# Retention with a gated output unit: output weights in whole rows, the fourth unit's states earlier, and 81 more TensorE products that move the blocks of its program

## The chip, the cores and the metric

The kernel runs on one core of a Trainium2 chip. The metric is the device time of one execution in microseconds (us), and less is better. Engines are named as in the profile: PE is TensorE's stream of matrix products and PEld its stream of weight loads; DVE, ACT, POOL and SP are the vector, scalar, GpSimd and sync engines. SP only issues transfers here.

## The reference

Eight batches, eight heads, 576 positions, head size 64; all inputs and the output are float32.

```python
scores = q @ k.T / sqrt(64)
ret = scores * Dmat             # gamma_h ** (i - j) for i >= j, else 0
x = (ret @ v), heads side by side          # 8 x 576 x 512
gate = sigmoid(causal depthwise convolution of x, 5 taps, conv_w)
out = (gate * (x @ w_val)) @ w_out         # 512 x 512 weights
```

## The kernel before

The work is cut into 18 units. Unit 2b and unit 2b+1 are the first and second 256 positions of batch b; units 16 and 17 hold the last 64 positions of four batches each. A unit's retention is done in chunks of 128 positions: inside a chunk by scores and a mask, from chunk to chunk by a 64x64 state for each head.

For one unit the steps are these. `load_half` and `load1` bring k, q and v as float32 tiles (`fk`, `fq`, `fv`, or `wkc`, `wqc`, `wvc` for units 0, 1, 16 and 17). `cast1` and `cast_half` (L237 to L268) make bf16 of them, on POOL for the most part. `turn` or `turn_halves` (L287) transposes k and q on PE into PSUM, from where ACT copies them into `kq` (L297). `scores` (L306) multiplies them, `masks` (L324) applies the mask on DVE, `carried` (L352) adds what the states bring, `values` (L380) multiplies with v, and `take_x` (L392) writes x. `update` (L411) multiplies k and v into the unit's part of the states (L425); ACT copies it out (`xf`, L433), and POOL makes the bf16 states from it (`s`, L436 to L450; in second units through `mid`, L447). `conv` (L475) is the convolution, 40 products of 64x64 weights with 256 columns, and a sigmoid on ACT (L497). `value` (L505) is x times w_val, eight products of 128x128 weights with 256 columns (L510); `gated` multiplies with the gate (L517). `project` (L521) is the product with w_out, four products with 512 columns for one half of a unit's rows (L526); ACT copies its result to `ob` (L529), and `store` sends a unit out.

The order is written out by hand, and each engine runs its own instructions in that order. Units 0 to 3 have an order of their own (L572 to L730). From unit 4 on a loop over n (L731) interleaves three units: it finishes the retention of n, runs conv, gate_values and project of n-1, and begins n+1. In one round PE has, in this order: carried and the second half of scores of n (24 products together in first units, whose first chunk has no state, and 32 in second ones), conv(n-1) (40), the first half of scores of n+1 (16), update(n+1) (32), values(n) (32), two gate_values (16), turn_halves (16), two projects (8). Two rounds, a first and a second unit, have 376 products. Each product is a weight load and a multiplication, two instructions of PE's program.

PSUM has four pools: `ps_a`, `ps_s` and `ps_o` with one buffer each, and `ps_v` with two. A tile takes a buffer only when its last reader is done.

Loads are held back by a touch: a tiny copy by DVE or ACT into the tile (L112, L131, L136, L137), behind which the transfer has to wait, so that SP issues it when that engine has come so far. SP issues in order, so a transfer that waits holds all behind it.

The output weights come as two tiles `wof`, each by two transfers to 64 partitions (L134), in pieces of 128 floats; `prep_wo` (L225) makes bf16 of them by four casts on POOL. It stands ahead of `update(3)`, so POOL does the four casts ahead of the states of unit 3, which `carried(3, 0)` (L695) needs.

Of the kernel before, what the change touches and what calls it, by code (L numbers as in the profile page):

```python
# [21 lines left out]
def kernel(  # L22
# [55 lines left out]
    with tc.manual_schedule():  # L78
# [46 lines left out]
        wof = [consts.tile([P, NP, 2, P], F32, name=f"wof{g}") for g in range(2)]  # L125
# [8 lines left out]
        def load_wo(g, touch):  # L134
            wo_src = moe_w_out.rearrange("(pr ab hl p) (n j) -> ab hl p n pr j", pr=2, ab=2, hl=2, j=P)
            touch(wof[g][0:1, 0, 0, 0:1], lsc[0:1])  # L136
            touch(wof[g][64:65, 0, 0, 0:1], lsc[64:65])  # L137
            for (p0, ab, hl) in (((0, 0, 0), (64, 1, 0)), ((0, 1, 1), (64, 0, 1)))[g]:
                nc.sync.dma_start(out=wof[g][p0:p0 + 64], in_=wo_src[ab, hl])
# [70 lines left out]
        def prep_conv():  # L210
            cps = ps_a.tile([P, KC * NP], F32, name="a")
            nc.tensor.transpose(cps, cwn, identf[0:KC * NP, 0:KC * NP])
            cw = small.tile([P, KC * NP], F32, name="cw")
            nc.vector.tensor_copy(cw, cps)
            nc.vector.tensor_tensor(
                dg.rearrange("p o k j -> p k o j"),
                cw.rearrange("p (k o) -> p k o", o=NP).unsqueeze(3).to_broadcast([P, KC, NP, 64]),
                id2.unsqueeze(1).unsqueeze(1).to_broadcast([P, KC, NP, 64]), op=ALU.mult)

        def prep_wv(e, eng):  # L220
            for (j0, ab, hl) in (((0, 0, 0), (64, 1, 0)), ((0, 1, 1), (64, 0, 1)))[e]:
                for pr in range(2):
                    eng(wvb[e][:, :, pr, j0:j0 + 64], wvf[2 * pr + ab][:, :, hl * 64:hl * 64 + 64])

        def prep_wo():  # L225
            for o in range(NP):
                nc.gpsimd.tensor_copy(wob[:, o, :].rearrange("p (g j) -> p g j", j=P), wof[o // 2][:, :, o % 2, :])

        def warm(n, cols=512, pool=None):
            z = (pool or ps_v).tile([P, 512], F32, name="s" if pool else "v")  # L230
            for i in range(n):
                nc.tensor.matmul(z[:, 0:cols], lhsT=zero[:, 0:P], rhs=zero[:, 0:cols], start=True, stop=True)
# [44 lines left out]
        def turn(u, pool, i):  # L277

            new_turned(u)
            ps = tps[u, i] = pool.tile([P, 2, 2, 2, P], BF16, name="v" if pool is ps_v else f"o{i}")  # L280
            for hf in range(2):
                for prl in range(2):
                    for r in range(2):
                        h = 2 * (2 * hf + prl)
                        nc.tensor.transpose(ps[:, hf, prl, r, :], bf[u]["kq"[i]][:, r, h:h + 2, :].rearrange("p h d -> p (h d)"), ident)  # L285

        def turn_halves(*pairs):  # L287
            ps = ps_a.tile([P, 2, 2, 2, 2, P], BF16, name="a")
            for (at, (u, hf)) in enumerate(pairs):
                for i in range(2):  # L290
                    for prl in range(2):
                        for r in range(2):
                            h = 2 * (2 * hf + prl)
                            nc.tensor.transpose(ps[:, at, i, prl, r, :], bf[u]["kq"[i]][:, r, h:h + 2, :].rearrange("p h d -> p (h d)"), ident)  # L294
            for (at, (u, hf)) in enumerate(pairs):
                new_turned(u)
                nc.scalar.copy(kqt[u][hf].rearrange("p i l r c a -> p (i l r c a)"), ps[:, at].rearrange("p i l r a -> p (i l r a)"))  # L297
# [8 lines left out]
        def scores(u, hf, between=None, pool=None):  # L306

            if pool is ps_v:
                s = [pool.tile([P, 2, 2, P], F32, name="v") for par in range(2)]
            else:  # L310
                st = (pool or ps_s).tile([P, 2, 2, 2, P], F32, name="a" if pool else "s")
                s = [st[:, par] for par in range(2)]
            t = kqt[u][hf]
            for prl in range(2):
                for r in range(2):
                    for (c, par) in QUAD:
                        nc.tensor.matmul(s[par][half[c], prl, r, :], lhsT=t[half[par], 0, prl, r, c, :],  # L317
                                         rhs=t[half[par], 1, prl, :, c, :],
                                         start=True, stop=True, skip_group_check=True)
                    if between and prl == 0 and r == 0:  # L320
                        between()
            sps[u, hf] = s if pool is ps_v else st
# [29 lines left out]
        def carried(u, odd, chs=(0, 1)):  # L352
# [3 lines left out]
            for pr in range(NP):  # L356
                t = kqt[u][pr // 2]
                for c in chs:
                    par = c ^ odd
                    rows = half[par]  # L360
                    if kind == "full":
                        st = state.get((b, 2 * cu + c))
                        if st is None:
                            continue
                        nc.tensor.matmul(o[c][rows, pr, :], lhsT=st[rows, pr, :],  # L365
                                         rhs=t[rows, 1, pr % 2, :, c, :],
                                         start=first(u, c, par), stop=False, skip_group_check=True)
                    else:
                        for i in range(2):
                            st = state[b + 2 * c + i, 4]  # L370
                            cs = slice(i * 32, i * 32 + 32)
                            nc.tensor.matmul(o[c][rows, pr, :].rearrange("p (r a) -> p r a", r=2)[:, :, cs],
                                             lhsT=st[rows, pr, :], rhs=t[rows, 1, pr % 2, :, c, cs],
                                             start=first(u, c, par), stop=False, skip_group_check=True)
# [5 lines left out]
        def values(u, hf):  # L380
# [3 lines left out]
            for prl in range(2):  # L384
                pr = 2 * hf + prl
                for r in range(2):
                    for (c, par) in QUAD:
                        nc.tensor.matmul(o[c][half[par], pr, :], lhsT=vb[half[c], 2 * pr + par, r, :],  # L388
# [22 lines left out]
        def update(u, own=False):  # L411
# [9 lines left out]
            for pr in range(NP):  # L421
                for r in range(2):
                    for (c, par) in QUAD:
                        h = 2 * pr + par
                        nc.tensor.matmul(xy[c][half[par], pr * 64:pr * 64 + 64], lhsT=kb[half[c], r, h, :],  # L425
# [9 lines left out]

            s1 = stp.tile([P, NP, 64], BF16, name="s1")  # L436
# [16 lines left out]

# [21 lines left out]
        def conv(j, i, gate=True):  # L475
            n, ss = width(j), sets(j, i)
            g = ps_a.tile([P, 2, len(ss), n], F32, name="a")
            for si, s in enumerate(ss):
                a, b = 2 * s, 2 * s + 1
                for kk in range(KC):  # L480
                    for (rows, blk, cols, bank) in ((lo, a, lo, 0), (hi, b, lo, 1), (lo, b, hi, 0), (hi, a, hi, 1)):
                        nc.tensor.matmul(g[cols, bank, si, :], lhsT=dg[rows, blk, kk, :], rhs=xs(j, rows, blk, kk),  # L482
# [22 lines left out]
        def value(j, i, e):  # L505
            n, ss = width(j), sets(j, i)
            vp = ps_v.tile([P, len(ss), n], F32, name="v")
            for si, s in enumerate(ss):
                for o in range(NP):
                    nc.tensor.matmul(vp[:, si, :], lhsT=wvb[e][:, o, s, :], rhs=xs(j, slice(0, P), o, PAD),  # L510
# [10 lines left out]
        def project(j, m, r, eng=None):  # L521
            u = jobs[j][m]
            o = ps_v.tile([P, DM], F32, name="v")
            for jj in range(NP):
                z = zsb[j][:, jj, m * W:(m + 1) * W].rearrange("p (a r) -> p r a", r=2)
                nc.tensor.matmul(o, lhsT=z[:, r, :], rhs=wob[:, jj, :], start=(jj == 0), stop=(jj == NP - 1))  # L526
# [4 lines left out]
        def last_rows(j):  # L531
# [5 lines left out]
            for jj in range(NP):  # L537
                for r in range(2):
                    nc.tensor.matmul(o[r], lhsT=z[:, jj, r, :], rhs=wob[:, jj, :], start=(jj == 0), stop=(jj == NP - 1))
# [42 lines left out]
        load_wv(0)  # L582
        turn(0, ps_o, 0)
# [28 lines left out]
        load_wv(1, act)  # L612
# [4 lines left out]
        load_wv(2, dve)  # L617
        scores(1, 1, pool=ps_a)
        masks(1, 1)
        load_wv(3, dve)  # L620
        load_half("k", 3, 0, dve)
# [3 lines left out]
        load_half("k", 3, 1, act)  # L625
# [8 lines left out]
        load_half("q", 3, 0, dve)  # L634
# [3 lines left out]
        load_half("q", 3, 1, dve)  # L638
# [3 lines left out]
        load_half("v", 3, 0, dve)  # L642
# [3 lines left out]
        load_half("v", 3, 1, dve)  # L646
        scores(2, 1, pool=ps_v)
        load_wo(0, dve)
        masks(2, 1)
        load_wo(1, dve)  # L650
        prep_wv(0, pool)
        conv(1, 0)
        update(2)
        prep_wv(1, act)
# [16 lines left out]
        prep_wo()  # L671
        conv(2, 0)
        cast1("q", 3, act)
        gate_values(1, 0)
        load_half("v", 4, 0, dve)
        gate_values(1, 1)
        load_half("v", 4, 1, dve)
# [4 lines left out]
        load_half("k", 5, 0, dve)  # L682
        update(3)
        cast1("k", 4)
        gate_values(2, 0)
        load_half("q", 5, 0, dve)
        gate_values(2, 1)
        prep_tail_mask()
        load_half("v", 5, 0, dve)
# [4 lines left out]
        load_half("v", 5, 1, dve)  # L694
# [3 lines left out]
        load_half("k", 5, 1, dve)  # L698
        load_half("q", 5, 1, dve)
        project(0, 0, 0)  # L700
        project(0, 0, 1)
        store(0)
        project(1, 0, 0)
        values(3, 0)
        values(3, 1)
# [4 lines left out]
        load_half("k", 6, 0, dve)  # L710
        load_half("q", 6, 0, dve)
        turn_halves((4, 0))
        project(1, 0, 1)
        store(1)
        scores(4, 0)
        masks(4, 0)
        cast1("v", 5)
# [4 lines left out]
        load1("v", 6)  # L722
        turn_halves((4, 1), (5, 0))
        load_half("k", 6, 1)
        load_half("q", 6, 1)
        project(2, 0, 0)
        project(2, 0, 1)
# [3 lines left out]
        for n in range(4, NU):  # L731
# [34 lines left out]
            project(n - 1, 0, 0)  # L766
            project(n - 1, 0, 1)
# [35 lines left out]
```

## Time and profile before

| | |
|---|---|
| runs, without a profile | 162.41 us median of 3 (162.15 to 164.02) |
| the profiled execution, its own time | 164.84 us |
| its span, first to last instruction | 163.1 us |
| PE | 145.4 us busy, 3380 products |
| DVE, ACT, POOL | 105.5, 90.2, 103.1 us busy |
| transfers | 40.36 MB, 247 GB/s over the span |

The profiled execution lies 2.4 us above the median of the runs, and above the slowest of them. Its busy times are sums over stages with different limits. The span is longer than any engine's busy time, so what counts in each stage is which wait ends last.

### The profile page before, as it was taken

How to read it: one execution, taken by the hardware profiler on the slowest of the kernel's cores; microseconds unless marked ns; L12 is line 12 of the kernel's file. 1: busy time of each engine (PE TensorE's matmuls, PEld its weight loads, DVE VectorE, ACT ScalarE, POOL GpSimd, SP SyncE). 2: the span in 40 equal slices, each digit the busy share in tenths (PEclk: the TensorE clock that was granted, in tenths of full speed). 3: DMA queues.
4: the chain of work that ended last, by engine and by line, in shares of the span. 5: the costliest groups of instructions: out<-in, count | busy, mean ns of one | idle time of the engine just before them, and what ended most of it. 6: DMA issues, size and time to landing. Idle time of an engine off the chain costs nothing.

```text
span 163.1 us, 7863 instructions
## 1 busy us (share of the span) xinstructions
PE 145.4 (89%) x3380; PEld 107.9 (66%) x3380; DVE 105.5 (65%) x221; ACT 90.2 (55%) x160; POOL 103.1 (63%) x168
## 2 busy tenths in 40 slices
PE   6987978959999699996999999988999999999970
PEld 1556655835587578685769687867786877867530
DVE  4886896585466666665666676856676767664550
ACT  6795651816775528462847557474738483652420
POOL 7567764789969691969296959694949672400000
PEclk9999999999999999999999999999999999999997
DMA  4999899899999999897889898998899892303134
GB/s 125 347 346 341 252 299 231 240 295 304 323 341 354 330 324 289 250 316 216 250 255 305 270 285 253 300 274 284 227 244 277 227 285 113 133 4 133 26 103 129
DMA packets 64288, 40.36 MB, mean 247 GB/s; under 512 B 2410, under 2 KB 61822, under 8 KB 64254
## 3 DMA queue, kind: packets, MB, share of 16 engines
q1 hardware_dynamic: 64032, 39.59, 79.9%
q8 instruction: 26, 0.43, 1.2%
q10 hardware_dynamic: 222, 0.27, 0.7%
q14 instruction: 8, 0.07, 0.1%
HBM read 30.42 MB, written 9.44 MB: 244 GB/s over the span
## 4 chain that ended last, share of the span: by engine, by line
PE 72%; DVE 10%; issue 6%; DMA 3%; POOL 3%; SPq 2%; ACT 2%; DVEq 0%; POOLq 0%; ACTq 0%
PE v L510 19%; PE v L526 15%; PE a L482 10%; PE a L294 7%; PE o L388 4%; PE o L365 3%; PE s L425 3%; DVE p L334 3%; PE s L317 2%; SPq L97 2%; DMA wqc<-in_q_dram 2%; PE v L317 2%; DVE p L330 2%; PE o L285 1%; DVE xg L399 1%
## 5 line engine op out<-in xcount | busy, mean ns | idle before, releaser
L297 ACT COPY kq<-a 128x1024 bf16<-128x1024 bf16 x28 | 27.1, 1015 | 35.8 <-PE a L294 35.8
L510 PE MATMUL v<-xg,wvb 128*128 128x256 bf16 x288 | 35.2, 273 | 4.2 <-issue 3.9
L517 DVE TENSOR_TENSOR z<-gate,v 128x512 bf16<-128x512 f32 x34 | 23.3, 686 | 18.6 <-PE v L510 17.4
L334 DVE TENSOR_TENSOR p<-s,mask 128x1024 bf16<-128x1024 f32 x17 | 20.8, 1222 | 19.5 <-PE s L317 19.5
L510 PEld LDWEIGHTS <-wvb 128*128 128x128 bf16 x288 | 26.7, 97 | 9.5 <-issue 4.9
L526 PE MATMUL v<-wob,z 128*128 128x512 bf16 x136 | 32.4, 379 | 0.2 <-DVE z L517 0.2
L245 POOL TENSOR_TENSOR vb<-fv,gin 128x512 bf16<-128x512 f32 x28 | 28.7, 1044 | 2.5 <-DMA fv<-in_v_dram 2.4
L497 ACT ACTIVATE gate<-a 128x1024 f32<-128x1024 f32 x17 | 17.4, 1025 | 17.2 <-PE a L482 10.6
L482 PE MATMUL a<-xg,dg 64*64 64x256 bf16 x720 | 24.3, 270 | 0.6 <-DVE xg L399 0.3
L399 DVE TENSOR_TENSOR xg<-o,gout 128x512 bf16<-128x512 f32 x32 | 22.2, 735 | 3.3 <-PE o L388 2.6
L529 ACT COPY ob<-v 128x512 f32<-128x512 f32 x34 | 18.5, 582 | 4.5 <-PE v L526 4.5
L526 PEld LDWEIGHTS <-z 128*128 128x128 bf16 x136 | 12.3, 98 | 13.0 <-DVE z L517 1.3
L482 PEld LDWEIGHTS <-dg 64*64 64x64 bf16 x720 | 19.9, 106 | 1.4 <-issue 0.9
L317 PEld LDWEIGHTS <-kq 64*64 64x64 bf16 x576 | 15.5, 106 | 2.6 <-issue 1.8
L252 POOL CAST kb<-fk 128x512 bf16<-128x512 f32 x28 | 17.0, 613 | 0.0
L330 DVE TENSOR_TENSOR p<-v,mask 128x512 bf16<-128x512 f32 x24 | 15.5, 686 | 1.1
L447 POOL TENSOR_TENSOR mid<-run,xf 128x256 f32<-128x256 f32 x8 | 5.8, 725 | 15.3 <-ACT xf L433 13.6
L388 PE MATMUL o<-p,vb 64*64 64x128 bf16 x576 | 12.4, 218 | 1.8 <-DVE p L334 0.6
L252 POOL CAST qb<-fq 128x512 bf16<-128x512 f32 x22 | 13.5, 616 | 0.1
L317 PE MATMUL s<-kq 64*64 64x128 bf16 x304 | 12.2, 222 | 0.7 <-ACT kq L297 0.3
L388 PEld LDWEIGHTS <-vb 64*64 64x64 bf16 x576 | 9.8, 107 | 3.6 <-issue 3.2
L365 PEld LDWEIGHTS <-s 64*64 64x64 bf16 x192 | 7.0, 106 | 7.7 <-issue 2.5
(104 smaller groups left out, 201.7 us busy)
## 6 DMA issues: line engine op xcount, KB each, us to landing
out_dram<-ob SPq DMA_DIRECT2D x16, 512.0 KB, 5.0
fk<-in_k_dram SPq DMA_DIRECT2D x28, 256.0 KB, 4.4
fq<-in_q_dram SPq DMA_DIRECT2D x28, 256.0 KB, 4.9
fv<-in_v_dram SPq DMA_DIRECT2D x28, 256.0 KB, 4.9
wkc<-in_k_dram SPq DMA_DIRECT2D x2, 512.0 KB, 4.9
wqc<-in_q_dram SPq DMA_DIRECT2D x2, 512.0 KB, 5.4
wvc<-in_v_dram SPq DMA_DIRECT2D x2, 512.0 KB, 5.9
wvf<-in_moe_w_val_dram SPq DMA_DIRECT2D x4, 256.0 KB, 3.7
```

What stands on the lines that cost most here:

```text
L245: nc.gpsimd.tensor_tensor(b[n][:, hs].rearrange("p h r d -> p (h r) d"), f.rearrange("p h (r d) -> p (h r) d", r=2), gin[:, units[u][2], h ...
L252: (eng or nc.gpsimd.tensor_copy)(b[n][:, :, hs].rearrange("p r h d -> p h r d"), f.rearrange("p h (r d) -> p h r d", r=2))
L297: nc.scalar.copy(kqt[u][hf].rearrange("p i l r c a -> p (i l r c a)"), ps[:, at].rearrange("p i l r a -> p (i l r a)"))
L317: nc.tensor.matmul(s[par][half[c], prl, r, :], lhsT=t[half[par], 0, prl, r, c, :], rhs=t[half[par], 1, prl, :, c, :], start=True, stop=Tru ...
L330: nc.vector.tensor_tensor(p[:, par].rearrange("p l r a -> p l (r a)"), sps[u, hf][par].rearrange("p l r a -> p l (r a)"), mrow.to_broadcas ...
L334: nc.vector.tensor_tensor(p.rearrange("p e l r a -> p (e l) (r a)"), sps[u, hf].rearrange("p e l r a -> p (e l) (r a)"), mrow.to_broadcast ...
L388: nc.tensor.matmul(o[c][half[par], pr, :], lhsT=vb[half[c], 2 * pr + par, r, :], rhs=p[half[c], par, prl, r, :], start=first(u, c, par), s ...
L399: nc.vector.tensor_tensor(x[:, b, :, PAD + i0:PAD + i0 + P].rearrange("p o (a r) -> p o r a", r=2), o[c].rearrange("p o (r a) -> p o r a", ...
L482: nc.tensor.matmul(g[cols, bank, si, :], lhsT=dg[rows, blk, kk, :], rhs=xs(j, rows, blk, kk), start=(si == 0 and kk == 0), stop=(si == len ...
L510: nc.tensor.matmul(vp[:, si, :], lhsT=wvb[e][:, o, s, :], rhs=xs(j, slice(0, P), o, PAD), start=(si == 0 and o == 0), stop=(si == len(ss) ...
L517: nc.vector.tensor_tensor(zsb[j][:, 2 * e + ss[0]:2 * e + ss[-1] + 1, :], gsb[j, i][e], vps[j, i, e], op=ALU.mult)
L526: nc.tensor.matmul(o, lhsT=z[:, r, :], rhs=wob[:, jj, :], start=(jj == 0), stop=(jj == NP - 1))
```

## The change

Six things are changed.

1. The output weights are loaded as four tiles of 128 partitions, each row 512 floats long, and cast by ACT (two) and POOL (two). So that each block of 128 rows fits, the second bank of the convolution has its two blocks on the other partitions, and the order of a group of four conv products is now lower-lower, upper-upper, lower-upper, upper-lower. `prep_wv` follows.
2. `update` can leave its POOL part for later (`states`). For unit 3 that part now stands behind one cast of output weights instead of four.
3. `project` takes `split`: for the first `split` of its four weight blocks the 512 columns are done in two products of 256. All products are counted, and `fill()` adds small products on zeros (64 columns) until the count, with 16 added, leaves 50 when divided by 127.
4. Around unit 4 the order is another: `turn_halves` for (4, 0) comes before `project(1, 0, 0)`, in a `ps_v` buffer, and the one for (4, 1) and (5, 0) before scores(4, 0); `values(3, 1)` comes before `values(3, 0)`; the mask for the tail is made later.
5. Loads come earlier or without a touch in several places.
6. `prep_wv(1)`, the four casts of w_val on ACT, moves ahead of `conv(1, 0)`.

PE has 3461 products after it: 73 from splits and 8 from `fill()`. In the loop, `split` is 2 and 2 for even n and 2 and 1 for odd n, so that two rounds have 383 products.

```diff
-        wof = [consts.tile([P, NP, 2, P], F32, name=f"wof{g}") for g in range(2)]
+        wof = [consts.tile([P, DM], F32, name=f"wof{o}") for o in range(NP)]
...
+        def load_wo(o, touch=None):
+            if touch:
+                touch(wof[o][0:1, 0:1], lsc[0:1])
+            src = moe_w_out.rearrange("(pr ab hl p) n -> hl pr ab p n", pr=2, ab=2, hl=2)
+            nc.sync.dma_start(out=wof[o], in_=src[o // 2, o % 2])
+
+        made = [0]
+        BLOCK, PLACE = 127, 50
...
+        def fill():
+            z = ps_v.tile([P, 512], F32, name="v")
+            while (made[0] + 4 * NP) % BLOCK != PLACE:
+                matmul(z[:, 0:64], lhsT=zero[:, 0:P], rhs=zero[:, 0:64], start=True, stop=True)
...
-            for (j0, ab, hl) in (((0, 0, 0), (64, 1, 0)), ((0, 1, 1), (64, 0, 1)))[e]:
+            for (j0, ab, hl) in (((0, 0, 0), (64, 1, 0)), ((0, 0, 1), (64, 1, 1)))[e]:
...
-        def prep_wo():
-            for o in range(NP):
-                nc.gpsimd.tensor_copy(wob[:, o, :].rearrange("p (g j) -> p g j", j=P), wof[o // 2][:, :, o % 2, :])
+        def prep_wo(os, eng):
+            for o in os:
+                eng(wob[:, o, :], wof[o])
...
         def turn_halves(*pairs):
-            ps = ps_a.tile([P, 2, 2, 2, 2, P], BF16, name="a")
+            if len(pairs) == 1:
+                ps = ps_v.tile([P, 1, 2, 2, 2, P], BF16, name="v")
+            else:
+                ps = ps_a.tile([P, 2, 2, 2, 2, P], BF16, name="a")
...
+            xfs[u] = xf
+            if now:
+                states(u)
...
-                    for (rows, blk, cols, bank) in ((lo, a, lo, 0), (hi, b, lo, 1), (lo, b, hi, 0), (hi, a, hi, 1)):
+                    for (rows, blk, cols, bank) in ((lo, a, lo, 0), (hi, b, hi, 1), (lo, b, hi, 0), (hi, a, lo, 1)):
...
-                nc.tensor.matmul(o, lhsT=z[:, r, :], rhs=wob[:, jj, :], start=(jj == 0), stop=(jj == NP - 1))
+                n = DM // 2 if jj < split else DM
+                for c in range(0, DM, n):
+                    matmul(o[:, c:c + n], lhsT=z[:, r, :], rhs=wob[:, jj, c:c + n], start=(jj == 0 and c == 0),
+                                     stop=(jj == NP - 1), skip_group_check=True)
...
         masks(2, 0)
-        load_half("v", 3, 1, dve)
+        load_wo(0, dve)
+        load_wo(1)
         scores(2, 1, pool=ps_v)
-        load_wo(0, dve)
         masks(2, 1)
-        load_wo(1, dve)
+        load_wo(2, dve)
+        load_wo(3)
         prep_wv(0, pool)
+        prep_wv(1, act)
         conv(1, 0)
         update(2)
-        prep_wv(1, act)
...
-        prep_wo()
+        cast1("q", 3, act)
         conv(2, 0)
-        cast1("q", 3, act)
...
-        update(3)
+        update(3, now=False)
+        prep_wo((0, 1), act)
+        prep_wo((2,), pool)
+        states(3)
+        prep_wo((3,), pool)
         cast1("k", 4)
...
-        project(0, 0, 0)
-        project(0, 0, 1)
+        project(0, 0, 0, 4)
+        project(0, 0, 1, 4)
         store(0)
-        project(1, 0, 0)
+        turn_halves((4, 0))
+        project(1, 0, 0, 4)
+        values(3, 1)
         values(3, 0)
-        values(3, 1)
...
         update(4)
         take_x(3)
...
-        turn_halves((4, 0))
-        project(1, 0, 1)
+        turn_halves((4, 1), (5, 0))
+        project(1, 0, 1, 4)
         store(1)
         scores(4, 0)
...
-        turn_halves((4, 1), (5, 0))
...
-        project(2, 0, 0)
-        project(2, 0, 1)
+        fill()
+        project(2, 0, 0, 4)
+        project(2, 0, 1, 4)
...
-            project(n - 1, 0, 0)
-            project(n - 1, 0, 1)
+            project(n - 1, 0, 0, 2)
+            project(n - 1, 0, 1, 2 - n % 2)
```

## The prediction

> **What bounds the kernel now.** I read the page first, then the waits, the chain and timelines of single stretches.
>
> ```profile
> PE 145.4 (89%) x3380; PEld 107.9 (66%) x3380; DVE 105.5 (65%) x221; ACT 90.2 (55%) x160; POOL 103.1 (63%) x168
> ...
> PE 72%; DVE 10%; issue 6%; DMA 3%; POOL 3%; SPq 2%; ACT 2%; DVEq 0%; POOLq 0%; ACTq 0%
> ...
> q8 instruction: 26, 0.43, 1.2%
> ```
>
> PE sets the end: 72% of the chain is its work. The time to be won is where it stands still. Two kinds of stop stand out, the first in the waits:
>
> ```profile
> PEld L510 <- issue: 4.9, 5, 1.8
> PE v L510 <- issue: 3.9, 3, 1.6
> PEld L365 <- POOL s L448: 2.2, 1, 2.2
> PE o L365 <- POOL s L448: 2.0, 1, 2.0
> ```
>
> "issue" means that nothing the profile shows was waited for. Laid beside the transfers, these stops have an owner. Queue q8 fetches 26 times 16 KB, and the longest stops lie behind such a fetch, here one that ran from 55.07 to 56.03 us (timeline: start, us, what, and in brackets the idle time before):
>
> ```profile
> 55.40 0.28 PE L510 MATMUL v<-xg,wvb 128*128 128x256 bf16 x1
> 57.30 0.92 PE L510 MATMUL v<-xg,wvb 128*128 128x256 bf16 x7 [1.62 <-issue]
> ```
>
> Counting the products from one stop to the next (stretch, us, busy time and number by engine, clock, transfer share, GB/s):
>
> ```profile
> 57.30:74.71 17.41, 15.79 (x384) 12.41 (x384) 11.35 (x22) 9.24 (x18) 12.53 (x20) 1.00 0.92 290
> 74.71:106.49 31.78, 31.07 (x768) 24.50 (x768) 22.25 (x43) 18.48 (x36) 23.81 (x37) 1.00 0.87 267
> ```
>
> From the restart at 57.30 us to the one at 74.71 are 384 products, to the one at 106.50 another 768: multiples of 128 products, 256 instructions, so 64 bytes each for 16 KB. PE's program comes in blocks of 128 products, and PE stops where the next block is not there yet. Beyond the usual spacing the four stops of the loop cost 1.80 (57.30), 1.75 (74.71), 0.79 (106.50) and 0.59 us (111.60), 4.9 in all; one at 26.45 costs 0.9.
>
> How long a block needs: over 17 blocks of the loop, the fetch begins 0.9 to 2.8 us after the first product of the block before, moves for 0.88 to 2.53 us, and at the stops PE goes on 1.27 to 1.52 us after it landed. With 1.3 us for the last, the sum is 3.3 to 5.1 us, mean 4.4, spread 0.5. Where PE does 128 products faster, it stops. Seven scores products, conv, 16 scores, update, values and one value product are 128 in 2.6 us: the stop at 57.30.
>
> The second kind is the 2.24 us before 35.87 (POOL's timeline):
>
> ```profile
> 31.60 1.17 POOL L227 CAST wob<-wof 128x512 bf16<-128x512 f32 x2 [0.62 <-DMA wof<-in_moe_w_out_dram]
> 33.51 1.17 POOL L227 CAST wob<-wof 128x512 bf16<-128x512 f32 x2 [0.74 <-DVE fq L112]
> 34.64 0.72 POOL L447 TENSOR_TENSOR mid<-run,xf 128x256 f32<-128x256 f32 x1
> 35.42 0.40 POOL L448 CAST s<-mid 128x256 bf16<-128x256 f32 x1
> ```
>
> POOL casts all output weights and waits twice for them, while `xf` has been there since 32.38.
>
> **The change, part by part.** The sum is made against the profiled execution (164.84 us, span 163.1); its saving is then taken off the median of 162.41, which lies 2.4 lower.
>
> *States of unit 3.* After it, POOL does one cast (0.61), then `mid` (to the start of `s` 0.78) and `s` (0.40). `xf` allows `mid` from 32.4, so `s` is ready at about 33.6, when carried wants it (33.63): minus 2.2. If the third weight transfer lands where the fourth did (33.36), `s` comes at 35.2: minus 0.65. I take 2.0, because the transfers should be quicker. From 26 to 30 us all transfers together move 182 GB/s, from 46 to 54 338; in the slow stretch two of the four loads to 64 partitions are issued. With 128 partitions 4 us at the full rate would move 0.6 MB more, 1.8 us earlier for what follows.
>
> What is late next: ACT, whose next casts wait for q of unit 4.
>
> ```profile
> 35.20 0.62 ACT L252 CAST qb<-fq 128x512 bf16<-128x512 f32 x1 [2.81 <-DMA fq<-in_q_dram]
> 36.77 0.62 ACT L252 CAST qb<-fq 128x512 bf16<-128x512 f32 x1 [0.96 <-DMA fq<-in_q_dram]
> ```
>
> Its two weight casts (0.62 each) fit into the 2.81. But behind these casts stand the copies of `project` to `ob`, which free `ps_v`, which the moved turn_halves(4, 0) now needs, at about 36.1 (the first project at 36.66 less 2.2, and 1.73 for two). The touch for the second half of q is at 27.90, its transfer was issued at 31.12 and landed at 36.70; after the change it lands between 33.5 (touch plus 5.57 of flight) and 36.7. At 35 it costs about nothing.
>
> *Order around unit 4.* PE waited 0.47 us at 41.99 for a `kq` copy; turned earlier, the copy is there: minus 0.4. New small waits, on `ob` copies and on the casts of unit 5, whose cover shrinks from 2 us to 1: plus 0.3 (0 to 0.8).
>
> *Extra products.* A product of 256 columns follows the last every 108.4 ns (L510), one of 512 every 216 (L526): a split costs 1 ns if its weight load is hidden as in L510. 73 of them: plus 0.1. If the loads were not hidden, 73 x 98 ns = 7.2. The Trainium skill speaks against it: TensorE: Matmul & The Clock Gate, Part 3, says that a weight load overlaps a running product only when its row group differs, and all these have all rows. The 108.4 ns with a load before each product disagree, and the measurement decides. Eight fills of 64 columns: plus 0.2, by a quarter of 108.4 ns each.
>
> *Conv places.* 40 products take 1.04 to 1.12 us, 27 ns each, a quarter of 108.4: four blocks work at once already, before and after. Nothing, within 0.04 for each of 18.
>
> *Touches left out, `prep_wv` earlier.* DVE saves 0.25 us ahead of masks(2, 1), but the stop at 26.45 behind them is set by its fetch (landed 24.70) and swallows it. The ACT casts go into ACT's 2.8 us of idle before 22.2. Nothing; if that fetch is quicker, up to minus 1.2.
>
> *Blocks at other places.* Two rounds are now 383 products, three blocks less one, so the borders stay put: one in conv (product 27 to 32 of 40), one in project (product 3 to 8 of 12), one at the start of values. Without stops, by the durations before: conv to project 4.55 us, growing to 5.2; values to conv 6.2; project to values 4.03, 3.95, 3.85, 3.64, 3.44 in turn, since the border creeps by a product each time. The four old stops go, minus 4.9. New ones come where a block needs longer. One block in the trace before begins at project with loads running: its fetch is at 124.22 to 125.15, need 3.9; the mean of all is 4.4. I take 4.1 with the spread of 0.5, which gives stops of 0.24, 0.28, 0.35, 0.51 and 0.68 before values, 0.1 elsewhere: 2.2. Bounds: 0 and 8.2 (every block needs 5.1).
>
> Sum: -2.0 - 0.4 + 0.3 + 0.1 + 0.2 - 4.9 + 2.2 = -4.5 us. From 164.84 that is 160.3 with a profile, and 157.9 without.
>
> The rest of the loop has cover for a PE that is early: transfers are busy to 89%, and POOL waits 1.4 us or more in most rounds for ACT.
>
> **The rivals.**
>
> *PE's program is read far ahead.* Then a border in project, whose slow products leave time, costs nothing. For it: the fetch at 143.96 begins 0.44 us before its block's first product, in project too. Against: there transfers were nearly over, and blocks that begin in transposes still saw 2.3 and 2.6. New stops 0: 162.41 - 6.7 = 155.7. The Trainium skill gives TensorE a queue of 64 instructions (TensorE: Matmul & The Clock Gate, its first table), which favours this; the average lag of 1.7 us, against 2.1 right after a stop, shows only a little of it.
>
> *q of unit 4 still lands at 36.7.* The `ob` copies begin at 37.4 and turn_halves at 38.0 instead of 36.1: 1.9 of the 2.0 are lost, 159.8.
>
> *The stops are not the fetches' doing* and come back elsewhere: 162.41 - 1.8 = 160.6. The Trainium skill (Runtime: NRT & Kernel Launch, Instruction fetch mechanics) has crossing a 16 KiB border mostly hidden, which is this case. Against it stand five stops exactly at borders, each after a late fetch.
>
> *Fetches need 5.1 us, and the change is slower.* Blocks at 106.50 and 111.60 needed 5.0 to 5.1, with transfers running as they will in project. Then five borders before values cost 1.1 to 1.7 each and those in project 0.2 to 0.5: 8.2 for 4.9, and with -1.8 from the rest 163.9. It decides from a mean need of 4.93 on. Against: only four of 17 needed that much.
>
> *Split loads are not hidden:* 157.9 + 7.2 = 165.1. Against it stands L510.
>
> **How the numbers follow.** Forecast 0.45; read ahead 0.20; late q 0.13; fetch needs 5.1 0.14; stops not the fetches' 0.05; split loads 0.03. The likeliest is 157.9. Two per cent, about what a measurement of this kernel can tell from no change, is 159.2 below and 165.7 above. The forecast is below with 0.8, reading ahead with 0.95, late q with 0.3: 0.59 faster. Slower by over 2%: a quarter of the fetch case and half of the split case, some 0.05. The range goes from just under the read-ahead case to just under the slower one: 154.9 to 163.4.
>
> **What would show it.** In the changed profile PE should wait for `s` no more than 0.6 us near 34; products of 256 columns in project should be 108 to 110 ns apart; the stops called issue should lie at values, five of 0.2 to 0.7 us, and none at 1.5 or more in value. Stops over 1 us at values, or in project, would make the prediction wrong, as would a wait of turn_halves on `ob` near 36, or stops away from borders 128 products apart.

## The result: slower by 8.3%

| | before | after |
|---|---|---|
| median of 4 runs each | 163.22 us (162.15 to 164.30) | 176.96 us (176.50 to 180.15) |
| ratio, 95% interval | | 1.083 (1.072 to 1.0945) |
| span of the profiled execution | 163.1 us | 175.2 us |

Ratios here and below come from runs within 1.5% of the fastest of their kernel, so a median over all runs and its ratio can differ, by up to 1.2 per cent.

The prediction, 157.9 us, has the wrong sign, and 176.96 lies outside its range. The page of after, in the lines that answer to those shown of before, and with two rows of the 40 slices (4.4 us each):

```profile
PE 149.5 (85%) x3444; PEld 118.3 (68%) x3461; DVE 105.1 (60%) x214; ACT 92.3 (53%) x162; POOL 102.8 (59%) x166
...
PEclk9999999985557999999999999999999999999999
...
GB/s 142 347 346 334 292 238 58 55 75 136 200 296 309 319 308 317 320 295 299 290 254 291 299 281 272 282 273 263 315 232 235 232 262 245 67 68 121 7 120 120
...
q8 instruction: 27, 0.44, 1.1%
...
PE 71%; DVE 9%; SPq 5%; issue 5%; DMA 4%; POOL 3%; ACT 1%; POOLq 0%; ACTq 0%; DVEq 0%
```

From the seventh to the ninth slice, 26 to 39 us, the transfers fall from over 300 GB/s to 55 to 75; from the tenth slice to the twelfth PE's clock is at a half. SP's queue has 5% of the chain and transfers 4%, against 2% and 3% before. The waits of after (engine, line, releaser; sum, times, longest; every product has line 146 now, that of the counting wrapper):

```profile
PEld L146 <- issue: 16.5, 42, 1.4
...
POOL wob L242 <- DMA wof<-in_moe_w_out_dram: 14.6, 2, 11.8
ACT qb L267 <- DMA fq<-in_q_dram: 14.4, 3, 11.9
...
PEld L146 <- POOL s L475: 10.1, 1, 10.1
...
PE o L146 <- POOL s L475: 10.0, 1, 10.0
```

PE's wait for `s` of unit 3, 2.2 us before, is 10.0 us. POOL's timeline says why (start, us, what, idle before):

```profile
41.24 0.61 POOL L242 CAST wob<-wof 128x512 bf16<-128x512 f32 x1 [11.79 <-DMA wof<-in_moe_w_out_dram]
41.82 0.72 POOL L474 TENSOR_TENSOR mid<-run,xf 128x256 f32<-128x256 f32 x1
42.60 0.40 POOL L475 CAST s<-mid 128x256 bf16<-128x256 f32 x1
...
46.45 0.61 POOL L242 CAST wob<-wof 128x512 bf16<-128x512 f32 x1 [2.77 <-DMA wof<-in_moe_w_out_dram]
```

The states follow the third cast, as the change wants, and that cast waits for the third weight transfer, which was issued at 23.75 and landed at 41.12. Transfers behind it wait too, on SP's queue (the time is that of the issues):

```profile
22.39 10.52 SPq L138 DMA_DIRECT2D wof<-in_moe_w_out_dram  x4
33.00 7.41 SPq L113 DMA_DIRECT2D fk<-in_k_dram  x2
40.50 3.67 SPq L113 DMA_DIRECT2D fq<-in_q_dram  x2
```

Four transfers of 256 KB keep SP for 10.5 us, so k, q and v of unit 4 come 12.5 to 13.3 us later than before (the second half of q at 49.24 instead of 36.70). On PE this makes three stops in a row; two smaller ones of the loop, 60 us apart, stand below them:

```profile
43.05 0.42 PE L146 MATMUL o<-kq,s 64*64 64x128 bf16 x4 [9.99 <-POOL s L475]
...
47.11 2.29 PE L146 MATMUL v<-wob,z 128*128 128x256 bf16 x10 [1.18 <-POOL wob L242]
50.47 0.58 PE L146 MATMUL v<-ident,kb 128*128 128x128 bf16 x4 [1.07 <-ACT ob L558]
...
70.18 0.22 PE L146 MATMUL s<-vb,kb 64*64 64x64 bf16 x2 [0.86 <-issue]
...
130.77 0.63 PE L146 MATMUL o<-p,vb 64*64 64x128 bf16 x30 [0.51 <-issue]
```

The ledger of the two profiled executions: `carried(4, 0)` begins at 59.4 us instead of 45.1, 14.4 lost. The waits account for 10.0 + 1.2 + 1.1, less the 2.2 that PE waited for `s` before: 10.1. The rest, 4.3, is about what the half clock cost, at which PE came back from its 10 us of idling and ran until about 55 us: up to `carried(4, 0)` PE is busy for 42.5 us against 37.5, with 32 products more (stretch, us; busy time and number for PE, weight loads, DVE, ACT and POOL; clock, transfer share, GB/s; after, then before):

```profile
0.00:59.45 59.45, 42.46 (x813) 30.65 (x816) 30.19 (x83) 30.03 (x50) 33.19 (x63) 0.86 0.73 222
```

```profile
0.00:45.07 45.07, 37.54 (x781) 25.18 (x781) 30.84 (x90) 27.47 (x47) 33.59 (x64) 1.00 0.97 283
```

From `carried(4, 0)` to the end of the span, after takes 115.8 us and before 118.0: 2.3 less. This is not shown to be the change's doing, for the second profile of the unchanged kernel, at the end of the experiments, takes 115.8 there too.

**Why are these transfers slow?** For each of before's weight transfers the trace has 16 updates of its semaphore, one for each landing. For each of after's it has three: one as the transfer is issued (23.47, 24.08, 25.59 and 33.33 us), which would have to stand for 14 of the 16, and then two landings, at 30.51 and 30.82, 35.66 and 35.94, 40.85 and 41.12, 46.10 and 46.40: one transfer every 5.2 us. From 28 to 43 us some 2.1 packets of 2 KB are under way at any time. That is the picture of two DMA engines working for each transfer, one transfer after the other; which engines they are the trace does not tell. The source of a transfer has the dimensions 2 (`ab`), 64 and 512. The Trainium skill (DMA: Bandwidth & Descriptors, section "Why a DMA increments its semaphore by 16 and not by 1") has the rule for it: the hardware takes the largest number up to 16 that divides the slowest dimension of both sides, and the sequencer writes the counts of the engines left out at once. With a slowest dimension of 2 that makes two engines, and 14 counts at once: the trace agrees, with two landings and one update at the issue.

### The profile page after: what moved, and what is told of

Same layout as the page of the kernel before. It is cut to its first block, busy times and chain, and to the rows that moved or that the text cites. A ratio compares the mean times of both kernels' runs of the same rounds, so it can differ in the third digit from the quotient of the medians.

```text
span 175.2 us, 7992 instructions
## 1 busy us (share of the span) xinstructions
PE 149.5 (85%) x3444; PEld 118.3 (68%) x3461; DVE 105.1 (60%) x214; ACT 92.3 (53%) x162; POOL 102.8 (59%) x166
## 4 chain that ended last, share of the span: by engine, by line
PE 71%; DVE 9%; SPq 5%; issue 5%; DMA 4%; POOL 3%; ACT 1%; POOLq 0%; ACTq 0%; DVEq 0%
PE v L146 39%; PE a L146 16%; PE o L146 10%; PE s L146 7%; SPq L113 5%; DVE p L352 4%; DMA fq<-in_q_dram 4%; DVE p L348 1%; DVE z L543 1%; DVE xg L417 1%; DVE kq L319 1%; POOL vb L260 1%; POOL qb L267 1%; POOL kb L267 1%; DVE last L570 0%
## 5 line engine op out<-in xcount | busy, mean ns | idle before, releaser
L315 ACT COPY kq<-a 128x1024 bf16<-128x1024 bf16 x26 | 25.0, 1015 | 29.4 <-PE a L146 29.4
L146 PE MATMUL v<-wob,z 128*128 128x256 bf16 (+1 forms) x195 | 34.6, 317 | 2.5 <-POOL wob L242 1.2
L146 PEld LDWEIGHTS <-z 128*128 128x128 bf16 x217 | 21.3, 103 | 10.6 <-issue 2.5
L146 PEld LDWEIGHTS <-kb 64*64 64x64 bf16 (+1 forms) x656 | 16.4, 109 | 7.0 <-issue 2.8
L146 PE MATMUL o<-kq,s 64*64 64x128 bf16 (+1 forms) x256 | 11.7, 219 | 10.0 <-POOL s L475 10.0
L146 PEld LDWEIGHTS <-s 64*64 64x64 bf16 x256 | 8.6, 110 | 16.3 <-POOL s L475 10.1
L146 PEld LDWEIGHTS <-kq 64*64 64x64 bf16 x576 | 16.0, 107 | 2.0 <-issue 1.5
L146 PE MATMUL o<-p,vb 64*64 64x128 bf16 x576 | 13.0, 223 | 1.7 <-issue 0.5
L474 POOL TENSOR_TENSOR mid<-run,xf 128x256 f32<-128x256 f32 x8 | 5.8, 728 | 12.5 <-ACT xf L451 11.0
```

What stands on the lines that cost most here:

```text
L146: return f(*a, **k)
L474: nc.gpsimd.tensor_tensor(mid, state[b, "run"], xf[:, 0], op=ALU.add)
```

## The experiments

**First set: two engines, or something else?** The theory says that the shape of the source costs the whole loss. Its rival is the new order (loads of values and weights ahead of others, states elsewhere), or the form to 128 partitions with rows of 2 KB. Four runs. (Beside the three sets of experiments, before has medians of 162.46, 162.91 and 162.50 us.)

The change with the load in halves:

```diff
-            nc.sync.dma_start(out=wof[o], in_=src[o // 2, o % 2])
+            for ab in range(2):
+                nc.sync.dma_start(out=wof[o][half[ab]], in_=src[o // 2, o % 2, ab])
```

> The change with one edit: each of the four output weight tiles is loaded by two transfers to 64 partitions instead of one to 128. Theory (each of the four transfers ran on two of the 16 DMA engines, because its source has a slowest dimension of 2; all else of the change is sound): the semaphores of these loads show 16 landings each again, the four tiles are there by about 32 us instead of 46, PE's wait of 10 us for s of unit 3 is gone and so is the half clock from 43 to 57 us. After's front lost 14.4 us against before (product 812 begins at 59.45, product 780 of before at 45.07); without that loss, and with the 2.3 us that the loop gained, 158 to 161 us. Rival (the new order of the loads or the states, or rows of 2 KB, made the front late): 170 us or more, with the wait for s still above 4 us.

Measured: 161.93 us (median of 10), ratio to before 0.9975 (0.992 to 1.003). It is 15.0 us faster than after, PE does not wait for `s` at all, and `carried(4, 0)` begins at 45.3. It is above the 158 to 161 expected; PE's and SP's timelines show a new stop:

```profile
37.03 0.38 PE L147 MATMUL v<-ident,kb 128*128 128x128 bf16 x4 [2.07 <-ACT ob L559]
```

```profile
22.70 6.67 SPq L139 DMA_DIRECT2D wof<-in_moe_w_out_dram  x8
```

Eight issues take SP 6.7 us, so q of unit 4 comes late (at 35.80; 34.02 in the base of the second set), ACT casts it late, and the copies to `ob` behind these casts free `ps_v` late for `turn_halves(4, 0)`. This is the mechanism of the rival "q of unit 4 still lands at 36.7", and nearly its price: 2.07 against 1.9.

The change with other cuts of the rows, so that only the slowest dimension differs (4 blocks of 32 rows, and 16 blocks of 8; the rows meet other channels, so these two kernels compute another result):

```diff
-            src = moe_w_out.rearrange("(pr ab hl p) n -> hl pr ab p n", pr=2, ab=2, hl=2)
-            nc.sync.dma_start(out=wof[o], in_=src[o // 2, o % 2])
+            src = moe_w_out.rearrange("(a o p) n -> o a p n", a=4, o=NP)      # a=16 in the second
+            nc.sync.dma_start(out=wof[o], in_=src[o])
```

> The change with the rows of the output weights taken in another order, so that each transfer's source is 4 blocks of 32 rows (same size of 256 KB, same rows of 2 KB, one transfer to 128 partitions; the weights' rows thus meet other channels and the result is another). Theory: four DMA engines for each transfer, so 2.6 us for each instead of 5.2, four landings in each semaphore, the four tiles there by about 35 us; PE waits for s some 1 to 3 us, and the time is 159 to 165. Rival (packets of 2 KB or one transfer to 128 partitions are slow by themselves): as after, 174 to 179 us.

Measured: 165.0 us (median of 4), ratio 1.018 (1.004 to 1.033). Each semaphore now has one update at the issue and then four landings; the transfers land at 28.64, 31.59, 34.33 and 37.29, some 2.9 us apart. PE waits 3.5 us for `s`, a little more than the 1 to 3 expected.

> As the run with blocks of 32 rows, but with 16 blocks of 8 rows: still one transfer of 256 KB to 128 partitions for each tile, rows of 2 KB, and again the weights' rows meet other channels. Theory: 16 engines, 16 landings, about 1 us for each transfer when nothing else runs; time as with two transfers to 64 partitions, within 1.5 us (158 to 161). Rival (the single transfer to 128 partitions, or its 2 KB rows): 170 us or more.

Measured: 160.59 us (median of 10), ratio 0.990 (0.985 to 0.996), no wait for `s`, and the last of the four lands at 31.43. Same transfers, same rows, same order of work; what moves with the time is the slowest dimension alone. One stretch shows it best (stretch, us; busy time and number for PE, weight loads, DVE, ACT and POOL; clock, transfer share, GB/s), first for 2 (after), then for 4, then for 16:

```profile
30.00:34.00 4.00, 3.07 (x74) 2.39 (x70) 3.11 (x8) 2.08 (x4) 0.00 (x0) 1.00 0.15 55
```

```profile
30.00:34.00 4.00, 2.76 (x68) 2.12 (x65) 3.11 (x7) 2.32 (x5) 0.00 (x0) 1.00 0.44 150
```

```profile
30.00:34.00 4.00, 4.00 (x74) 3.31 (x73) 3.27 (x8) 2.37 (x5) 3.58 (x7) 1.00 1.16 322
```

The kernel before with that load and nothing else of the change:

```diff
+            src = moe_w_out.rearrange("(pr ab hl p) n -> hl pr ab p n", pr=2, ab=2, hl=2)
...
+            for pr in range(2):
+                nc.sync.dma_start(out=wof[2 * g + pr], in_=src[g, pr])
```

> The kernel before with nothing changed but the load of the output weights, which has after's form: four transfers, each with a source of two blocks of 64 rows, to 128 partitions (two of the four tiles then hold their halves the other way round). Theory (the load alone): each transfer on two engines, 21 us for the four; POOL, which casts all four tiles ahead of the states of unit 3, gets the last at about 48 us and PE waits more than 10 us for s: 174 to 180 us. Rival (the loads' or the states' new order does it): within 2% of before.

Measured: 176.5 us (median of 4), ratio 1.091 (1.081 to 1.100). The load alone makes the kernel before as slow as the whole change does (two of the tiles hold their halves the other way round, so the result is another here too). Its waits:

```profile
PEld L364 <- POOL s L447: 15.8, 1, 15.8
PE o L364 <- POOL s L447: 15.7, 1, 15.7
...
POOL wob L226 <- DMA wof<-in_moe_w_out_dram: 13.8, 3, 4.7
```

With POOL casting all four tiles ahead of the states, PE waits 15.7 us, where the change, with one cast ahead, waited 10.0. As to the transfers the theory holds in all four, and the rival is out; the one time outside its range, that of the halves, has the stop above.

**Second set: why the rest is worth so little.** With 16 engines the change should have made 157.9. It makes 160.6 to 161.9, so 2.7 to 4.0 us of the forecast are still missing. The base of the next runs is a better cut of the load, four transfers with two rows for each of 64 partitions:

```diff
+            g, ab = o // 2, o % 2
+            src = moe_w_out.rearrange("(pr ab hl p) n -> hl ab p pr n", pr=2, ab=2, hl=2)
+            nc.sync.dma_start(out=wof[g][half[ab]], in_=src[g, ab])
```

> The change, with the four transfers of the output weights cut the other way: each brings 64 partitions with two rows of 2 KB, so the slowest dimension is 64, the number of transfers stays four and SyncE's issues stay short. Theory (two DMA engines were the whole loss; the halves' run lost some 1.8 us again because SyncE spent 6.7 us on eight issues and q of unit 4 came late): all 16 engines, no wait for s of unit 3, the stop of 2.3 us before turn_halves(4, 0) shrinks to about 0.6, and the time is 159 to 161, 1 to 3 us below before. Rival (transfers to 64 partitions are slow here whatever the rows): the stop before turn_halves stays above 1.5 us and the time at 162.

Measured: 161.95 us (median of 6), ratio 0.995 (0.990 to 0.9999). The stop at `turn_halves(4, 0)` is gone (0.6 was expected); the time is not lower than in halves. PE waits for `s` again, which was not expected (the line below), and the stops at the borders in the loop sum to 3.3 us, where the halves' profile had 0.2:

```profile
PE o L147 <- POOL s L476: 1.1, 1, 1.1
```

The base without the extra products:

```diff
-                n = DM // 2 if jj < split else DM
+                n = DM
...
-        fill()
```

> The run before it (four transfers to 64 partitions with two rows each) without the split products and without the fills, so that the borders of PE's 128-product blocks stand where they stood in the kernel before. Theory of the prediction (the stops at the borders are fetches that come late, and their places decide): the stops of 1.5 us or more in value come back, 4 to 5 us in all against 2 to 3 with the places kept, and the time rises by 1.5 to 3.5 us. Rival (places do not matter): the time falls by 0.3 us, the price of the extra products, or stays.

Measured: 161.3 us (median of 6), ratio 0.989 (0.983 to 0.9945), not above the base. Its profiled execution has stops of 3.0 us at the borders in the loop, at the old places, 2.3 of them in `value`. The theory's 1.5 to 3.5 us do not show.

The base with POOL casting all four tiles ahead of the states:

```diff
-        prep_wo((0, 1), act)
-        prep_wo((2,), pool)
+        prep_wo((0, 1, 2, 3), pool)
         states(3)
-        prep_wo((3,), pool)
```

> The run with four transfers to 64 partitions and two rows each, but POOL casts all four weight tiles ahead of the states of unit 3, as in the kernel before. Theory (order on POOL): s is ready about 1.5 us later than PE wants it, PE waits for it 1 to 2 us and the time rises by 1 to 2 us. Rival (the early transfers alone remove the wait): no wait for s over 0.3 us, and no change.

Measured: 162.26 us (median of 6), ratio 0.984 (0.976 to 0.993). PE waits 2.2 us for `s` in the profile, 1.1 more than the base's; the times do not tell the two apart. The rise of 1 to 2 us that was expected does not show.

The kernel before with the split products and the fills alone, as in the change:

```diff
+        fill()
-        project(2, 0, 0)
-        project(2, 0, 1)
+        project(2, 0, 0, 4)
+        project(2, 0, 1, 4)
...
-            project(n - 1, 0, 0)
-            project(n - 1, 0, 1)
+            project(n - 1, 0, 0, 2)
+            project(n - 1, 0, 1, 2 - n % 2)
```

> The kernel before with the blocks' places alone: the split products and the fills of the change, nothing else of it. Theory of the prediction: the four stops of 57 to 112 us (4.9 us) turn into stops of some 2.2 us in all, the extra products cost 0.3, so the time falls by 2.4 us, 1 to 3.5; the waits for s of unit 3 (2.2 us) and for a kq copy at 42 us stay. Rival (places do not matter): 0 to +0.5 us.

Measured: 163.06 us (median of 6), beside 162.91 for before; ratio 0.996 (0.989 to 1.002). The stops at the borders of the loop sum to about 1.4 us in its profile, yet nothing comes out in the time that can be told from zero. So the term for the places was wrong. Is it the sizes, or the idea?

**Third set: places, and a second look at before.** First the base with the borders 24 products later in the work (the first four calls of `project` alike):

```diff
-        project(0, 0, 0, 4)
+        project(0, 0, 0)
...
-        fill()
```

> The run with four transfers to 64 partitions and two rows each, without the fills and without the split products of units 0 and 1: 24 products fewer ahead of the loop, so every border falls 24 products later in the work, and the dense stretch of scores, conv, scores, update and values (128 products in 2.4 us by the profile of the halves' run) is one whole block. Theory (fetches come late and places decide): with needs of 3.8 to 5 us, each of the five dense blocks of the loop ends in a stop of 1.2 to 2.5 us, 6 to 11 us in all where the run it comes from had 3.1 in its profile; the time is 164 to 169. Rival (the sum of the stops does not depend on the places): 160.5 to 163.

Measured: 164.96 us (median of 6), ratio 1.020 (1.012 to 1.028), 2.5% above the base's. Every dense block ends in a stop; three of the five:

```profile
55.23 0.35 PE L147 MATMUL o<-p,vb 64*64 64x128 bf16 x10 [0.63 <-issue]
...
71.36 0.35 PE L147 MATMUL o<-p,vb 64*64 64x128 bf16 x9 [1.07 <-issue]
...
87.14 0.31 PE L147 MATMUL o<-p,vb 64*64 64x128 bf16 x8 [0.72 <-issue]
```

So the idea holds: by the times, places can cost some 4 us. The sizes do not: the five stops are 0.67 to 1.34 us by the weight loads, 4.9 in all, where 6 to 11 were expected. That is only 1.5 us more than the base's 3.3; `carried(4, 0)` begins 1.2 later than in the base, and the two profiled executions, 164.10 and 161.43 us, do not lie further apart.

Then the base with the borders 8 products earlier:

```diff
-        BLOCK, PLACE = 127, 50
+        BLOCK, PLACE = 127, 58
```

> The run with four transfers to 64 partitions and two rows each, with eight more fills, so that every border falls 8 products earlier in the work. By the profile of the halves' run the blocks of the loop then take 4.3 to 6.2 us, where the shortest took 3.8. Theory (fetches and places): a block that needs 4.4 us just fits, the stops in the loop sum to 0 to 1.5 us, and the time falls by 0.5 to 2.5, to 159.5 to 161.5. Rival (places do not matter): +0.2 us for the fills.

Measured: 161.67 us (median of 12), ratio 0.989 (0.982 to 0.996). Blocks of 4.3 us and more do not help: its profile still has three large stops at borders, 2.0, 0.7 and 0.6 us, outside the 0 to 1.5 expected. The rival's reading, no difference, fits better.

On top of it the states ahead of both POOL casts:

```diff
-        prep_wo((2,), pool)
         states(3)
-        prep_wo((3,), pool)
+        prep_wo((2, 3), pool)
```

> The run with eight more fills, and the states of unit 3 on POOL ahead of both of its weight casts (ACT keeps the first two). Theory: POOL no longer waits for the third weight transfer before the states, s is ready at 32.3, PE's stop of 1.1 to 2.5 us for s goes, project then waits up to 0.5 us for the last casts; 0.5 to 1.5 us below the run with eight more fills, 158.5 to 160.5. Rival (q of unit 4 sets the front anyway, through the ob copies behind its casts on ACT): the stop moves to turn_halves(4, 0) and the time stays within 0.5 us.

Measured: 160.67 us (median of 12), ratio 0.9915 (0.9865 to 0.9965): the lowest median among the kernels that keep the weights' rows in place, and below both kernels, though its ratio cannot be told from those of the run before it, the run without places (0.989) or the run with four casts first (0.984). The step did what it was for. POOL's timeline:

```profile
31.06 0.73 POOL L475 TENSOR_TENSOR mid<-run,xf 128x256 f32<-128x256 f32 x1 [2.77 <-ACT xf L452]
31.85 0.40 POOL L476 CAST s<-mid 128x256 bf16<-128x256 f32 x1
...
32.88 1.16 POOL L243 CAST wob<-wof 128x512 bf16<-128x512 f32 x2
```

`s` is there at 32.2 and `carried(3, 0)` begins at 32.24, without a wait; `carried(4, 0)` begins at 42.6 instead of 45.5 (43.1 in the base). The stops in the loop, 3.4 us, are as large as in the base.

Last, the kernel before as it is, for a second profile:

> The kernel before, unchanged, for a second profile. Theory A (the stops at the borders belong to the places): the same four stops at values and value products again, 4 to 5.5 us in all. Theory B (how late a fetch is differs from one execution to the next, and the profiled execution, 2.4 us over the median, was a bad one): stops at the same borders but of other sizes, 1 to 3.5 us in all.

Measured: 164.37 us, once. The stops of the loop, in PE's timeline:

```profile
58.30 1.80 PE L510 MATMUL v<-xg,wvb 128*128 128x256 bf16 x15 [0.86 <-issue]
...
74.69 0.49 PE L510 MATMUL v<-xg,wvb 128*128 128x256 bf16 x3 [0.55 <-issue]
...
90.97 0.33 PE L294 MATMUL a<-ident,kb 128*128 128x128 bf16 x3 [0.50 <-issue]
```

Beyond the usual spacing that is 1.0, 0.7 and 0.7 us, and with one of 0.3 at 126 us 2.7 in all, where the first profile had 4.9. Two stops stand at the same borders, the two at 106 and 112 us are missing, and those at 91 and 126 us are new. Theory B: the stops of one execution are not those of the next. But this execution is as slow as the first with 2.2 us less of stops: its `carried(4, 0)` begins at 46.8 us, 1.8 later.

## Why the prediction was wrong, point by point

*Weight load: the step that failed.* "I take 2.0, because the transfers should be quicker": no load of before had a slowest dimension of 2, and its weight transfers have 16 landings each. One load did show that the landings follow the shape: `cwn`, 20 rows to 20 partitions, has one update at 1.51 us, as its issue ends, and then ten landings, which fits the rule (10 is the largest number up to 16 that divides 20). The prediction looked at partitions (64 against 128) and row lengths, and carried the full rate over; at worst it had the third transfer land at 33.36 and `s` come at 35.2. Measured: 55 GB/s instead of 338, 5.2 us for each of four transfers, one behind the other, the third landing at 41.12 and `s` at 43.0. Cutting the same load otherwise takes the kernel from 176.96 to 160.6 to 161.95, so this one step is 15.0 to 16.4 of the 19.1 us by which the forecast missed. It was not among the rivals, and no rival let a transfer become slower; the range's upper end, 163.4, was set by stops of PE.

*States of unit 3, minus 2.0.* The mechanism was right as to the wait; its size hung on the landing of the third transfer. With 16 engines PE's wait for `s` is 0 (halves; 16 blocks), 1.1 (base), 2.3 (without places) and 2.1 us (even places), against 2.2 with the states behind four casts. The prediction had the other bound, 0.65 if the third lands late, and took the better one. With the states ahead of both POOL casts nothing hangs on a transfer, and the wait is 0. That the time falls by what the wait loses is not shown: neither the base and four casts first (0.995 and 0.984) nor even places and states first (0.989 and 0.9915) can be told apart.

*Late q of unit 4.* Right in kind as a rival: 2.07 us in the run with halves, where it landed at 35.80.

*Order around unit 4, extra products, conv places.* Right. The wait for a `kq` copy near 42 us is gone in the base; products of 256 columns in `project` follow each other every 109 ns; a fill takes 29 ns; 40 conv products in the loop take some 1.0 to 1.1 us in both kernels.

*Blocks at other places, minus 4.9 plus 2.2.* The borders were right to the product: after's stops in the loop stand at the weight loads 1118, 1886, 2270 and 2654, all 94 more than a multiple of 128, and sum to 2.4 us. That this is close to the 2.2 is luck: six profiles with the same program on PE have 0 (four blocks), 0.2 (halves), 2.4 (after), 3.3 (base), 3.5 (16 blocks) and 3.7 us (four casts first), counting stops of 0.15 us and more. The minus 4.9 was mis-sized. It was measured in one execution that lay 2.4 us above the median, and then taken off that median: three other executions with borders at the old places have 1.4 (before with the load), 2.7 (the second profile of before) and 3.0 (without places). No profile of before at its median is on record, so how much of such stops the median pays stays open. The stops are all that varies in this part: from `carried(4, 0)` to the end the fourteen profiles take 113.4 to 118.1 us, and without the stops 113.0 to 113.5. What the places were worth is within what these runs can tell from zero (base against no places; before against before with places). That a block needs 4.1 us, give or take 0.5, was wrong in kind: a fetch begins 0.3 to 1.2 us after the first load of a dense block that follows a long one, and 1.5 to 3.5 us after that of the block behind it. What did hold is the end of each stop: at those of 0.4 us and more in the profiles of before, base, even and dense places, PE goes on some 1.2 to 1.5 us after the fetch has landed.

*Rivals on the fetches.* "Read far ahead" is out: the base stops 0.85 us at a border in `project`. "Not the fetches' doing" is out by the dense places. "Need of 5.1": single blocks needed up to 6.2, but not as a rule. "Split loads not hidden" is out by the 109 ns.

Why one execution has no stops in the loop (four blocks) and another 3.7 us of them (four casts first), with the same program on PE, stays open.

## What to carry to other kernels

Before a transfer is recut, look at the slowest dimension of both of its access patterns as well as at partitions and bytes: with a slowest dimension of 2 each transfer here had two landings instead of 16 and took 5.2 us, and all that was queued behind it waited. The number of landings in a trace tells it. A stop that was measured in one profiled execution may only be taken off that execution's time; before it is taken off a median, see it in a second profile. Work that a late transfer can hold up should not stand ahead of work that needs none.

## What the runs showed of the hardware

- The rate of a transfer with a slowest dimension of 2, 4 and 16: one 256 KB transfer every 5.2, 2.9 and about 1.2 us; 55, 150 and 322 GB/s for all transfers from 30 to 34 us.
- SP's queue stands behind such transfers: the fourth issue took 7.7 us, where three of the four take 0.6 in the base.
- After 10 us without products PE ran at half clock (transposes 0.61 us instead of 0.39) for some 12 us, in which it stopped twice more. After shorter waits it is not the same in every execution: 6.8 us of half clock followed a wait of 3.5 us (four blocks) and 3.4 us stops of 2.1 to 2.4 (halves, without places, the second profile of before), none waits of 2.0 to 2.8 (before, even places, four casts first, before with places).
- In the run with dense places the fetch comes 0.3 to 1.2 us after the border where the block is dense, and 1.5 to 3.5 us after the next border: the dense blocks, 2.4 us of work, cost 0.7 to 1.3 us each, and not the 2 us of a fixed need of 4.4.
